# First layer of a three-way maximum network: seven half products in place of eight for seven of nine pairs of feature blocks

## The chip, the cores and the metric

The kernel runs on one core of one Trainium2 chip. The metric is the device time of one execution in microseconds (us); shorter is better. TensorE multiplies; VectorE (DVE), ScalarE (ACT) and GpSimd (POOL) do the elementwise work; SyncE (SP) issues the loads and stores.

## What is computed

```python
# q, k, v: 2 x 8 heads x 768 tokens x 64; local causal window of 96 tokens and 8 global tokens
scores = where(keep, q @ k.T / 8 - slope * dist, -1e9)
x = softmax(scores) @ v                       # 1536 tokens x 512
# first layer: three weights of 512 x 768, then 768 x 512
h = maximum(maximum(x @ w1, x @ w2), x @ w3)
x = h @ w_out
# gated layer: root mean square norm, two weights of 512 x 1536, then 1536 x 512
xn = x / sqrt(mean(x * x) + 1e-6) * rms_g
out = (silu(xn @ w_gate) * (xn @ w_val)) @ w_out2
```

The weights arrive in 64-bit floating point. Each number is held as a high and a low part, so every product of two blocks is three matmuls: low weight by high token, high by low, high by high.

## The kernel before

The 1536 tokens are two batches of 768, cut into four chunks of 384 columns (`C2`) for the first layer. The weights of a layer are cut into blocks of 128 features; a block holds 512 inputs as four pieces of 128 (`KT`).

**Attention** (`FastAttention.steps`) runs in 24 units of two heads by 256 queries. One step j of the loop issues for several units at once: the scaling of unit j+2 on POOL, the low part of unit j-1 (`out(..., True)`, a subtraction on DVE), scores of unit j+3 and transposes of unit j+1 on TensorE, the exponentials (maximum on DVE, exponential on ACT), the values of unit j on TensorE, and the high part of unit j (`out(..., False)`, ACT). PE, DVE, ACT and POOL keep the program's order here (`manual(FRONT)`). Into each step `fast` puts half units of the first layer (six matmuls: half of the 512 inputs of one weight block by one chunk), from step 12 on two in a step, and `w.pace` puts pieces of the conversion of weights.

**Weights** (`Weights`) are fetched by SP, turned from 64-bit to 32-bit by a scaling on ACT (`scaled`) and three bit operations on DVE (`bits`), and then either split into high and low (`split`, ACT and POOL) or kept whole for the gated layer (`pair`), where `operand` makes the sums of half blocks (DVE), their high part (ACT) and low part (POOL). `pace` advances this by one piece, and stops where the ring of `RING` split blocks is full.

**First layer** (`first`, `firsts`): for each block of 128 hidden features and each chunk, the products with the three weights come one after the other; the first is copied into `h1` by ACT, the two others enter by a maximum on DVE. Blocks 0 and 1 are begun inside attention, the rest follows in `behind`.

**Rows** (`rows`, `row_stage`, `square`, `power`, `scale`, `norm`): for each of 12 tiles of 128 tokens, 18 matmuls give the output product, ACT squares and sums it, DVE and POOL make the inverse root, DVE scales, TensorE transposes, and `norm` makes the operands of the gated layer in `xb`, seven of them for two tiles: Strassen's sums of tokens (features in halves, tokens in halves of a batch).

**Gated layer** (`gated`, `second`, `chained`): each pair of a gate block and a value block is one 2 x 2 block product by seven half products. `chained` sums them in three accumulators of two banks; DVE, ACT and POOL add, apply silu and multiply. `order` is written out by hand, and operands are made seven products ahead. A last product follows (`group_stage`, `stage`, `last`, `store`). In `behind` only TensorE keeps the program's order; DVE, ACT and POOL are ordered by a planner there.

## Time and profile before

| | us |
|---|---|
| median of 3 runs | 573.3 (572.76 to 573.45) |
| the profiled execution | 573.58 |
| its span, from the first to the last instruction | 571.8 |
| TensorE busy | 561.8 |
| DVE busy | 343.3 |
| ACT busy | 267.0 |
| POOL busy | 244.1 |

The table is read so: the span is what the profile covers, and the profiled execution's own time is 1.78 us more. Busy times of different engines overlap. A large busy share alone doesn't say what bounds a stage; for that the stages are read one by one.

### The profile page before, as it was taken

To read this page: it belongs to the slowest core of one execution; us is meant where nothing else is said; L and a number is where in the kernel's file an instruction comes from. 1 tells how busy PE (TensorE), PEld (TensorE's weight loads), DVE (VectorE), ACT (ScalarE), POOL (GpSimd) and SP (SyncE) were. 2 spreads that over 40 slices of the span, in tenths; PEclk is the share of its full clock that TensorE was granted. 3 is DMA by queue.
4 is the path that set the end of the run, shared out by engine and by line. 5 is a ranking of instruction groups with operands and counts; after the bars stand their busy time and mean duration, and the time that the engine had idled before them with its cause. 6 is when DMAs were issued, how large, how long until landed. Compare 5 with 4: busy or idle time off the path is not lost.

```text
span 571.8 us, 9171 instructions
## 1 busy us (share of the span) xinstructions
PE 561.8 (98%) x3324; PEld 508.8 (89%) x3324; DVE 343.3 (60%) x757; ACT 267.0 (47%) x628; POOL 244.1 (43%) x301
## 2 busy tenths in 40 slices
PE   8999999999999999999999999999999999999995
PEld 3778788899999999988899999999999998888884
DVE  5999889628679412267778555555556459752220
ACT  3888776514344001165755455555554546442210
POOL 4556554305155001057646666666666526420000
PEclk9999999999999999999999999999999999999999
DMA  8666663202535300000000222222222205303001
GB/s 297 192 207 225 216 216 105 80 1 80 179 83 190 97 1 0 1 2 1 1 0 1 75 73 75 76 73 75 75 73 75 73 1 155 104 2 128 33 24 42
DMA packets 15894, 48.72 MB, mean 85 GB/s; under 512 B 2016, under 2 KB 2016, under 8 KB 15840
## 3 DMA queue, kind: packets, MB, share of 16 engines
q1 hardware_dynamic: 15840, 48.05, 26.2%
q8 instruction: 28, 0.46, 0.3%
q14 instruction: 26, 0.21, 0.1%
HBM read 44.90 MB, written 3.15 MB: 84 GB/s over the span
## 4 chain that ended last, share of the span: by engine, by line
PE 90%; DVE 4%; ACT 3%; issue 1%; DMA 1%; POOL 0%; SPq 0%; DVEq 0%; ACTq 0%
PE c L574 28%; PE mm L379 27%; PE acc L638 17%; PE mo L426 8%; PE sc L844 3%; PE tr L885 3%; PE av L908 3%; ACT s L861 2%; DVE s L857 1%; PE tr L460 1%; DMA qk<-qk 1%; PE idle L369 1%; DVE xt L919 0%; DVE g L517 0%; ACT xb L464 0%
## 5 line engine op out<-in xcount | busy, mean ns | idle before, releaser
L574 PE MATMUL c<-xb,op 128*128 128x384 f32 x924 | 160.4, 334 | 0.2 <-DVE g L517 0.2
L574 PEld LDWEIGHTS c<-xb,op 128*128 128x128 f32 x924 | 160.1, 188 | 0.5 <-POOL op L254 0.5
L379 PE MATMUL mm<-xt,w 128*128 128x384 f32 x864 | 157.7, 338 | 0.0
L379 PEld LDWEIGHTS mm<-xt,w 128*128 128x128 f32 x864 | 148.5, 188 | 2.6 <-issue 2.6
L168 POOL TENSOR_TENSOR w<-x,w 128x512 fp32r<-128x512 f32 x36 | 51.8, 1441 | 79.7 <-ACT w L165 71.2
L875 POOL TENSOR_SCALAR s<-s,rs 128x232 f32<-128x232 f32 (+1 forms) x96 | 42.3, 459 | 37.5 <-DVE rs L870 27.7
L396 DVE TENSOR_TENSOR h<-mm,h 128x384 f32<-128x384 f32 x48 | 26.5, 553 | 46.9 <-PE mm L379 46.7
L426 PE MATMUL mo<-w,rst 128*128 128x512 f32 x216 | 52.1, 395 | 0.0
L861 ACT ACTIVATE s<-s,nmx 128x232 f32<-128x232 f32 (+1 forms) x96 | 44.5, 466 | 13.1 <-DVE nmx L857 12.8
L254 POOL TENSOR_TENSOR op<-s,op 128x256 fp32r<-128x256 f32 x48 | 38.1, 796 | 29.2 <-ACT op L253 28.0
L638 PE MATMUL acc<-w,gst 128*128 128x512 f32 x216 | 49.2, 389 | 0.0
L638 PE MATMUL acc<-w,st 128*128 128x512 f32 x216 | 49.1, 389 | 0.0
L638 PEld LDWEIGHTS acc<-w,st 128*128 128x128 f32 x216 | 40.6, 188 | 8.4
L638 PEld LDWEIGHTS acc<-w,gst 128*128 128x128 f32 x216 | 40.5, 188 | 8.4
L426 PEld LDWEIGHTS mo<-w,rst 128*128 128x128 f32 x216 | 39.8, 188 | 8.0
L588 POOL TENSOR_TENSOR h<-h,g 128x768 f32<-128x768 f32 x20 | 36.9, 1846 | 12.3 <-ACT g L607 10.0
L254 POOL TENSOR_TENSOR op<-x,op 128x256 fp32r<-128x256 f32 x36 | 29.1, 812 | 22.2 <-ACT op L253 22.2
L857 DVE CUSTOM_DVE_ANT_0 s<-sc,bias 128x232 f32<-128x232 f32 (+1 forms) x96 | 31.9, 376 | 6.8 <-PE sc L844 5.3
L610 DVE TENSOR_TENSOR h<-c,h 128x768 f32<-128x768 f32 x11 | 10.5, 958 | 41.9 <-PE c L574 41.9
L165 ACT CAST w<-x 128x512 fp32r<-128x512 f32 x36 | 22.2, 619 | 22.7 <-DVE x L151 14.6
L394 ACT COPY h<-mm 128x384 f32<-128x384 f32 x24 | 11.3, 472 | 42.4 <-PE mm L379 42.2
L844 PE MATMUL sc<-qk 64*128 64x232 f32 (+1 forms) x192 | 27.8, 379 | 2.4 <-DVE nmx L857 1.0
(114 smaller groups left out, 745.0 us busy)
## 6 DMA issues: line engine op xcount, KB each, us to landing
raw<-wgv SPq DMA_DIRECT2D x24, 512.0 KB, 3.8
raw<-w SPq DMA_DIRECT2D x18, 512.0 KB, 3.7
raw<-wo SPq DMA_DIRECT2D x18, 512.0 KB, 3.7
qk<-qk SPq DMA_DIRECT2D x24, 312.0 KB, 4.0
v<-vwin SPq DMA_DIRECT2D x10, 512.0 KB, 5.5
out<-o SPq DMA_DIRECT2D x12, 256.0 KB, 2.1
v<-vwin SPq DMA_DIRECT2D x2, 256.0 KB, 4.9
gcol<-gcol SPq DMA_DIRECT2D x1, 2.0 KB, 1.7
```

Source lines behind the costliest of these rows:

```text
L168: self.nc.gpsimd.tensor_tensor(out=t[:, 1, :], in0=self.x.pop(i), in1=t[:, 0, :], op=ALU.subtract)
L254: nc.gpsimd.tensor_tensor(out=t[:, 1, :], in0=s, in1=t[:, 0, :], op=ALU.subtract)
L379: self.nc.tensor.matmul(ps, w[:, wi, k * P:(k + 1) * P], x[b][:, k, xi, c0:c0 + C2], start=(i == 0), stop=(i == 3 * KT - 1),)
L396: self.nc.vector.tensor_tensor(out=h, in0=ps, in1=h, op=ALU.max)
L426: self.nc.tensor.matmul(ps, h[:, k % 3, hi, :], w[:, wi, :], start=(k + x == 0), stop=(k == NF1 - 1 and x == 2),)
L574: nc.tensor.matmul(two[:, b, :C2], a[:, wi, k * P:(k + 1) * P], self.xb[b][:, j, k, xi, :], start=(i == 0 and j in (0, 1, 5)), stop=(i == ...
L588: nc.gpsimd.tensor_tensor(out=o, in0=o, in1=y, op=ALU.mult)
L638: self.nc.tensor.matmul(ps, of(si), w[:, wi, :], start=(f == LAST[0] and si == 1), stop=(f == LAST[-1] and si == 0 and wi == 0),)
L844: nc.tensor.matmul(sc[j][:, i, :n], qk[r, i * P:(i + 1) * P], qk[r, k0:k0 + n], start=True, stop=True)
L857: nc.vector.tensor_tensor_reduce(out=s[:, j, :n], in0=self.sc[d][j][:, i, :n], in1=self.bias(n, 2 * pr + j), scale=-QK, scalar=3.0e38, op0 ...
L861: nc.scalar.activation(s[:, j, :n], s[:, j, :n], AF.Exp, bias=nmx[:, j:j + 1], scale=-1.0, accum_out=sm[:, i, j:j + 1])
L875: nc.gpsimd.tensor_scalar(s[:, j, :n], s[:, j, :n], rs[:, i, j:j + 1], 1.0, op0=ALU.mult, op1=ALU.mult)
```

## The change

In the first layer, four weight blocks of the first two feature blocks (the first two of the three weights) stay as plain products. The remaining weights are taken by pairs of neighbouring feature blocks: seven pairs, each a 2 x 2 block product (features in two blocks, inputs in halves, tokens in halves of a batch) by seven half products, in the same chained form that the gated layer has (`chained`, `sums1`). The sums of tokens that they need are made on chip from a 32-bit copy of attention's result (`xf`, `places`, `mix`, `mix_split`): for batch 0 during attention, for batch 1 behind it. `out` copies attention's result to `xf` on DVE, and its low part is now subtracted by POOL. The sums of half weight blocks for these pairs are made by POOL. FILL gives the half units per attention step, PACES the pieces of conversion per pair. The weights of the output product come in between (`couple`). The whole first layer keeps the program's order on all four engines. The first gated pairs' weights are now converted during the rows.

```diff
-RING = 9
+RING = 4
+NPLAIN = 2
+FILL = [0] * 12 + [1, 1, 2] * 4 + [2] * 4
+NA = 7
+PACES = [6, 14, 6, 6, 14, 8, 0]
...
     def pair(self, i):
+        f = self.units[i][0][1]
+        self.blocked = len(self.held) == 2
+        while self.blocked:
+            yield
+            self.blocked = len(self.held) == 2
+        self.held.add(f)
...
-            nc.vector.tensor_tensor(out=s, in0=x, in1=y, op=op)
+            (nc.gpsimd if -NA < f < 0 else nc.vector).tensor_tensor(out=s, in0=x, in1=y, op=op)
...
+        self.firstly = [(f, w) for f in range(0, NF1, 2) for w in range(NPLAIN if f == 0 else 0, 3)]
+        for n, (f, w) in enumerate(self.firstly):
+            for x in range(2):
+                u.append((("w1", n - NA, x), io["w123"][f + x, w], "op"))
+            for k in {3: (0, 1), 6: (2, 3, 4, 5)}.get(n, ()):
+                u.append((("wo1", k), io["wo1"][k], "wo1"))
...
-        for w in range(3):
+        for w in range(NPLAIN):
...
+    def tokens(self, j, b, k, x):
+        if j in (2, 3, 6):
+            if x == 0:
+                return self.thi[b][:, (2, 3, 6).index(j), k, :]
+            return self.xlo[b, j][:, k, :]
+        r, h = {0: (0, 0), 1: (1, 0), 4: (1, 1), 5: (0, 1)}[j]
+        return self.xt[b][:, 2 * r + k, x, h * C2:(h + 1) * C2]
+
+    def mix(self, b, j, eng):
+        q = self.xf[b]
+        o, x, y = {
+            3: ((0, 0), (0, 1), (0, 0)), 5: ((0, 1), (1, 1), (0, 1)),
+            2: ((1, 1), (1, 1), (0, 0)), 6: ((1, 0), (1, 0), (1, 1)),
+        }[j]
+        eng.tensor_tensor(out=q[o], in0=q[x], in1=q[y], op=ALU.subtract)
+
+    def mix_split(self, b, j, eng=None):
+        o = self.xf[b][MIXED[j]]
+        hi = self.xt[b][:, :2, 0, C2:] if j == 5 else self.thi[b][:, (2, 3, 6).index(j)]
+        if eng is None:
+            self.nc.scalar.copy(hi, o)
+            return
...
+        eng.tensor_tensor(out=lo, in0=o, in1=hi, op=ALU.subtract)
...
                 for wi, xi in ((1, 0), (0, 1), (0, 0)):
+                    x = self.tokens(j, b, k, xi) if f < 0 else self.xb[b][:, j, k, xi, :]
...
+    def sums1(self, n, j, ps):
...
+        if j == 0:
+            nc.scalar.copy(held(1), ps)
+        elif j == 1:
+            nc.vector.tensor_tensor(out=held(1), in0=ps, in1=held(1), op=ALU.add)
+            most(1)
+        elif j == 2:
+            nc.scalar.copy(held(2), ps)
+        elif j == 3:
+            nc.scalar.copy(held(3), ps)
+        elif j == 4:
+            if w == 0:
+                nc.scalar.copy(best[4], ps)
+            else:
+                nc.vector.tensor_tensor(out=best[4], in0=ps, in1=best[4], op=ALU.max)
+        elif j == 6:
+            nc.vector.tensor_tensor(out=held(2), in0=ps, in1=held(2), op=ALU.add)
+            most(2)
+        if j == (5 if last else 3):
+            nc.vector.tensor_tensor(out=held(3), in0=self.chain[n, 5][:, :, :C2], in1=held(3), op=ALU.add)
+            most(3)
...
+    def begin(self):
+        z, self.n_op = -1, 0
+        self.order = [(-NA, 0), (-NA, 1), (-NA, 2), (-NA, 5), (-NA, 3)]
+        for o in range(1 - NA, z):
+            self.order += [(o, 0), (o - 1, 4), (o - 1, 6), (o, 1), (o, 2), (o, 5), (o, 3)]
+        self.order += [(z, 0), (z - 1, 4), (z, 2), (z - 1, 6), (z, 3), (z, 5), (z, 1), (z, 6), (z, 4)]
+
+    def strassen(self):
...
+        for n, _ in enumerate(self.firsts(NC2 - 1)):
+            for fn, *args in todo[n]:
+                fn(1, *args)
+            if n % 2 and self.n_op < 7:
+                self.next_op()
...
+        for n, (o, j) in enumerate(self.order):
+            later.step()
+            for b, _ in enumerate(self.chained(o, j)):
+                if b == 0:
+                    self.next_op()
...
+                w.pace(paces - done)
...
+            if (o, j) == (-1, 1):
+                self.row_part(0, 0)
+        w.need(("wo1", NF1 - 1))
+        self.row_part(0, 1)
+        later.flush()
...
-    def out(self, d, low):
+    def out(self, d, part):
...
+        if part == 0:
+            nc.scalar.copy(o[:, 0], av)
+            for q, n, i in self.places(b, pr, c):
+                nc.vector.tensor_copy(q, av[:, i * P:i * P + n])
+        elif last:
+            nc.vector.tensor_tensor(out=o[:, 1], in0=av, in1=o[:, 0], op=ALU.subtract)
         else:
+            for q, n, i in self.places(b, pr, c):
+                a = slice(i * P, i * P + n)
+                nc.gpsimd.tensor_tensor(out=o[:, 1, a], in0=q, in1=o[:, 0, a], op=ALU.subtract)
...
-                            w.pace(1 + (r >= WMORE) + (r >= WMOST))
+                            w.pace(1 + (r in (8, 9, 10, 12, 14, 16)))
+                        if r >= len(FILL) - 5:
+                            body.next_op()
+                        for fn, j, eng in mixes.get(r - LEAD, ()):
+                            fn(0, j, eng)
```

`mixes` gives the four mixes of batch 0 to POOL at units 14 to 17, their high parts to ACT and their low parts to DVE (two) and POOL (two) at units 14 to 24; `todo` gives the mixes of batch 1 to DVE, and the splits to ACT, DVE (three of the low parts) and POOL (one). In `sums1`, `most` is a maximum between two tiles in SBUF on DVE, left out for the first weight of a block pair, and split by batch for the last pair.

## Rows read from the trace of the kernel before

**Rows 1.** The page's busy times: us, share of the span, instructions of each engine.

```profile
PE 561.8 (98%) x3324; PEld 508.8 (89%) x3324; DVE 343.3 (60%) x757; ACT 267.0 (47%) x628; POOL 244.1 (43%) x301
```

**Rows 2.** The chain of waits in order of time: start us, us, engine, line.

```profile
118.12 119.63 PE mm L379 x689
...
237.75 8.21 PE mo L426 x36
...
307.31 160.40 PE c L574 x924
```

**Rows 3.** Busy time by stage: stretch, its length, busy us, TensorE clock, DMA.

```profile
237.75:287.50 49.75, 49.75 (x239) 41.07 (x239) 30.14 (x67) 29.79 (x74) 30.16 (x29) 1.00 0.00 1
...
45.20:118.12 72.92, 72.92 (x600) 60.18 (x600) 58.21 (x194) 46.80 (x154) 34.77 (x62) 1.00 0.46 155
118.12:237.75 119.63, 119.63 (x691) 119.63 (x691) 63.15 (x96) 32.34 (x63) 30.21 (x24) 1.00 0.25 76
19.00:45.20 26.20, 25.05 (x241) 19.50 (x240) 24.65 (x103) 23.27 (x82) 14.49 (x32) 1.00 0.59 183
```

**Rows 4.** The same chain of waits, one full step of attention.

```profile
85.85 0.98 PE sc L844 x8
86.84 1.02 PE tr L885 x8
87.86 1.05 PE mm L379 x6
88.91 1.03 PE av L908 x16
89.94 1.24 PE mm L379 x6
```

**Rows 5.** Instructions by line and shape, DVE: count, busy us, mean ns, idle before.

```profile
L145 DVE SCALAR_TENSOR_TENSOR x<-raw,x 128x512 int32<-128x512 int32 x30 | 23.1, 774 | 0.6
...
L610 DVE TENSOR_TENSOR h<-c,h 128x768 f32<-128x768 f32 x11 | 10.5, 958 | 41.9 <-PE c L574 41.9
...
L919 DVE TENSOR_TENSOR xt<-av,xt 128x256 fp32r<-128x256 f32 x24 | 9.6, 399 | 5.5 <-ACT xt L921 5.5
...
L478 DVE TENSOR_SCALAR z<-tr,gcol 128x128 f32<-128x128 f32 x12 | 3.9, 340 | 0.0
...
L647 DVE COPY o<-acc 128x256 f32<-128x256 f32 x1 | 0.4, 425 | 13.6 <-PE acc L638 13.6
```

**Rows 6.** The same view, POOL.

```profile
L168 POOL TENSOR_TENSOR w<-x,w 128x512 fp32r<-128x512 f32 x36 | 51.8, 1441 | 79.7 <-ACT w L165 71.2 <-DMA raw<-wo 8.5
...
L254 POOL TENSOR_TENSOR op<-s,op 128x256 fp32r<-128x256 f32 x48 | 38.1, 796 | 29.2 <-ACT op L253 28.0
L588 POOL TENSOR_TENSOR h<-h,g 128x768 f32<-128x768 f32 x20 | 36.9, 1846 | 12.3 <-ACT g L607 10.0 <-DVE h L610 2.3
L875 POOL TENSOR_SCALAR s<-s,rs 128x232 f32<-128x232 f32 x80 | 36.7, 477 | 25.6 <-DVE rs L870 20.3 <-PE tr L885 5.3
```

**Rows 7.** Single lines, DVE: duration in ns, shortest, median and longest.

```profile
L151 DVE SCALAR_TENSOR_TENSOR x<-raw,x x30: 677/691/1669, 28.3 to 188.2; 128x512 int32<-128x512 int32 x30
L151 DVE SCALAR_TENSOR_TENSOR x<-raw,xs x30: 675/687/689, 314.4 to 503.7; 128x512 int32<-128x512 int32 x30
...
L621 DVE TENSOR_TENSOR gst<-h,gst x12: 949/957/1808, 462.4 to 505.5; 128x768 fp32r<-128x768 f32 x12
```

**Rows 8.** The timeline where the rows begin: start us, us, engine, line.

```profile
241.91 0.60 ACT L439 ACTIVATE x<-mo 128x512 f32<-128x512 f32 x1 [1.52 <-PE mo L426]
...
242.49 0.50 ACT L413 CAST rst<-h 128x384 fp32r<-128x384 f32 x1
...
243.45 0.75 DVE L450 TENSOR_SCALAR x<-mo,ri 128x512 f32<-128x512 f32 x1 [0.67 <-POOL ri L446]
...
244.50 0.56 DVE L415 TENSOR_TENSOR rst<-h,rst 128x384 fp32r<-128x384 f32 x1 [0.29 <-ACT rst L413]
...
245.79 0.60 PE L460 MATMUL tr<-ident,x 128*128 128x128 f32 x4
```

More of the change, by code (lines that the diff above doesn't have):

```diff
@@ L173, in everything @@
             self.fetch(i)
-        two = [i for i, u in enumerate(self.units) if u[2] == "op"]
-        yield from self.convert(0, two[0])
-        for i in two[::2]:
-            yield from self.pair(i)
-        yield from self.convert(two[-1] + 1, len(self.units))
+        a, n = 0, len(self.units)
+        while a < n:
+            place = self.units[a][2]
+            if place == "op":
+                yield from self.pair(a)
+            elif place == "wo1":
+                yield from self.couple(a)
+            else:
+                z = a
+                while z < n and self.units[z][2] not in ("op", "wo1"):
+                    z += 1
+                yield from self.convert(a, z)
+                a = z - 2
+            a += 2
     def convert(self, a, z):
@@ L396, in part @@
                 self.nc.vector.tensor_tensor(out=h, in0=ps, in1=h, op=ALU.max)
-        for w in range(3):
+        for w in range(NPLAIN):
             self.weights.need(("w1", f, w))
             self.later.step()
-            ps = yield from self.product(("w1", f, w), self.xt, c, f"mm_{f}_{c}_{w}")
+            bank = None
+            if c == NC2 - 1 and f == 1 and w == 1:
+                bank = self.twos[2].tile([P, 2, 512], F32, tag="m2", name="mm2")[:, 0, :C2]
+            ps = yield from self.product(("w1", f, w), self.xt, c, f"mm_{f}_{c}_{w}", bank)
@@ L417, in row_stage @@
-        self.rst[t] = st
+            self.row_part(t, x)
     def rows(self, t):
-        ps = self.bank(f"mo_{t}")
+        ps = self.single(f"mo_{t}")
         for k in range(NF1):
@@ L490, in second @@
         nc, later = self.nc, self.later
-        nm, n = f"{f}_{b0}_{j}", b1 - b0
+        nm = f"{f}_{b0}_{j}"
         a = self.weights["op", f, j]
-        two = self.two_banks("q_" + nm) if n == 2 else None
         for b in range(b0, b1):
             later.step()
-            ps = two[:, b, :C2] if two is not None else self.bank("q_" + nm, C2)
+            ps = self.single("q_" + nm, C2)
             i = 0
@@ L613, in chained @@
-        self.later(1, ready)
+        if j == 0:
+            g = self.ev["g1", f] = self.evp.tile([P, B, C2], F32, tag="ev", name=f"g1_{f}")
+            nc.scalar.copy(g, ps)
+        elif j == 1:
+            g = self.ev["g1", f]
+            nc.vector.tensor_tensor(out=g, in0=ps, in1=g, op=ALU.add)
+            nc.scalar.activation(g, g, AF.Silu)
+        elif j == 2:
+            nc.scalar.copy(h[:, 0], ps)
+        elif j == 3:
+            nc.scalar.copy(h[:, 1], ps)
+        if j == (5 if last else 3):
+            c = self.chain[f, 5][:, :, :C2]
+            nc.vector.tensor_tensor(out=h[:, 1], in0=c, in1=h[:, 1], op=ALU.add)
@@ L653, in store, with firsts @@
         self.nc.sync.dma_start(out=self.io["out"][t * P:(t + 1) * P, :], in_=o)
-    def firsts(self, f0, f1, c0, c1):
-        for f in range(f0, f1):
-            for c in range(c0, c1):
-                yield from self.first(f, c)
-    def behind(self):
-        w, later = self.weights, self.later
-        for _ in self.firsts(2, NF1, 0, NC2):
-            if ("x", 1) not in w.done:
-                w.pace()
-        later.flush()
+    def firsts(self, c):
+        for f in range(2):
+            yield from self.first(f, c)
@@ L1089, in fast @@
 def fast(tc, io, consts, nlf, ngf):
-    chunks = [(b, c) for b in range(B) for c in range(NCH)]
+    nc, chunks = tc.nc, [(b, c) for b in range(B) for c in range(NCH)]
     def manual(engines):
@@ L1108, in fast @@
+        body.begin()
+        with manual(FRONT):
+            with ExitStack() as c2:
+                body.warm_up(c2)
                 att = FastAttention(body, c2, Masks(tc, c2, nlf, ngf), chunks)
-                side, n_side, r = early(), 0, 0
+                side, r = early(), 0
                 for part in att.steps():
                     if part < 2:
-                        c = n_side // 12
                         for _ in range(WARMS[r] if r < len(WARMS) else 0):
                             body.keep_warm(r)
-                        if c < NC2 - 1 and r >= LEAD + 1 + NPAIR * -(-(c + 1) * C2 // CN):
-                            next(side)
-                            n_side += 1
+                        if part == 0:
+                            for _ in range(FILL[r]):
+                                next(side)
@@ L1124, in fast @@
+            body.open_behind()
+            body.strassen()
         with manual(BEHIND):
-            for n, _ in enumerate(side):
-                w.pace(n % 2)
-            for n, _ in enumerate(body.firsts(0, 2, NC2 - 1, NC2)):
-                w.pace(n % 2)
             body.behind()
@@ L1134, in general @@
 def general(tc, io, consts, nlf, ngf):
-    chunks = [(b, c) for b in range(B) for c in range(NCH)]
+    nc, chunks = tc.nc, [(b, c) for b in range(B) for c in range(NCH)]
     with ExitStack() as ctx:
```

323 lines of the change are left out of this document (211 added, 112 removed).

## The prediction

> **What bounds the kernel now.** I read the page's busy lines first, then the chain of waits in order of time, then the busy times by stage, and last the prices of single forms. TensorE is busy for 98% of the span [rows 1]. The chain shows the same as lengths: one unbroken run of first-layer matmuls from 118.12 to 237.75 us, then the rows of the first output product, and from 307.31 us one run of 160.40 us of half products for the gated layer [rows 2]; between the rows' end (287.5, [rows 3]) and that run lie some 20 us in which small steps alternate. So a matmul taken out of one of these runs shortens the span by its pitch, as long as nothing else becomes later. The reader should see two things in the stage table [rows 3]. TensorE is busy all the time from 45.2 us on, while DVE has 58.21 of 72.92 us in the second half of attention, 63.15 of 119.63 in the first layer and 30.14 of 49.75 in the rows: there is room, but not without end. And from 19.0 to 45.2 us DVE has 24.65 of 26.20 and ACT 23.27: there TensorE waits for them. The granted clock is 1.00 in these stages (its upper level, 2.4 GHz) and plays no part.
>
> **The matmuls taken out.** Before, 18 weight blocks x 4 token chunks x 12 matmuls are 864. After, four blocks stay plain (4 x 4 x 12 = 192) and seven pairs take 7 products x 2 batches x 6 = 84 each, 588: 780 in all, 84 fewer. Where do they leave? In the run after attention, 689 matmuls took 119.63 us [rows 2], 0.1736 us each; the gated layer's half products, which have the form that the new ones get (three two-bank accumulators, chained sums), took 160.40 us for 924, also 0.1736 [rows 2]. The form therefore costs nothing by itself. After: of 24 half units (six matmuls each) that FILL deals out, two come behind the last `av`, eight more belong to the last chunk, so 60 + 588 = 648 matmuls x 0.1736 = 112.5 us, 7.1 less than 119.6. Inside attention a full step is scores 0.98, transposes 1.02, half unit 1.05, values 1.03, half unit 1.24 [rows 4]; 29 half units lie before the last `av` now (689 of 864 matmuls come after it), 22 will, and 7 x (1.05 + 1.24)/2 = 8.0 us go. Together **-15.1 us**, a little more than 84 x 0.1736 = 14.6, because a half unit inside attention costs more than its pitch. This holds if TensorE stays the engine that is late everywhere. The rest is what takes that away.
>
> **Attention, first part (to 45 us).** DVE's subtraction for the low part (399 ns) becomes a copy to `xf`; the nearest rows are a copy of the same size out of PSUM at 425 ns and, for the third of the units whose tokens fall in two quarters, two of 340 ns [rows 5]. That is +0.03 or +0.28 us in a step of 3.4, some 0.9 us over nine steps that DVE bounds. The copy also waits for the values of its own step on TensorE, and the weight bits and the next reciprocal queue behind it. The subtraction goes to POOL at about 0.8 us [rows 6], behind the four scalings; POOL is at 14.49 of 26.20 us, so there is room. But a DVE operation with both sources in SBUF that meets a POOL operation stretches: 691 ns median against 1669 at most for one form of the bits [rows 7]. One pace fewer at step 11 gives back 0.6. Bounds 0 and +3 us; I take **+1.0**, near the counted copies, because ACT and DVE alternate there and one pays for the other.
>
> **Attention, second part.** A step with one half unit needs 0.98 + 1.02 + 1.05 + 1.03 = 4.08 us of TensorE in place of 5.32. DVE had 58.21 us for 72.92 there, 80% or 4.2 us of a 5.3 us step, with two or three paces in a step; a pace is about one bit operation (0.77, [rows 5]), so with one it needs some 3.4. ACT had 46.80 of 72.92 us [rows 3]. So TensorE stays just ahead. The four mixes on POOL (the form of 768 takes 1.85 us; [rows 6] has these prices) and the five first operands come on top, and POOL then has four scalings (4 x 0.48) + 0.80 + 1.85 = 4.6 us in steps of 4.1 to 5.1. Nothing waits for the mixes at once. Bounds 0 and +3 us; **+1.0**, for four steps in which POOL is a little long and its subtractions stretch DVE's bits.
>
> **The Strassen stage (102 us).** DVE, for a pair whose result goes through a maximum: three additions out of PSUM (958 ns, [rows 5]), one maximum out of PSUM and three between SBUF tiles, 7 x 0.958 = 6.7 us, and six bit operations with one side in PSUM (0.69 each, the second form of [rows 7]), 4.1: 10.8 of the pair's 84 x 0.1736 = 14.6 us. Over the stage: five such pairs' sums 33.5, two without maxima 5.7, sixteen converted blocks at 2.1 make 33: 72 of 102 us. POOL: 49 operand subtractions and 24 sums at 0.80 plus six at 1.44 [rows 6] make 67 us. Both fit. The tightest wait: product (o+1,1) starts in the bank that (o,4) filled, one product (12 x 0.1736 = 2.08 us) later; DVE needs 0.96 for that maximum and may have up to one 0.96 in front. It holds with little to spare. Bounds 0 and +6 (five pairs of 1.2 us, one stretched maximum each in front of such a release); **+1.0**, by the gated layer, whose run [rows 2] is the same chain without a pitch above 0.1736 us, but with fewer DVE sums.
>
> A row first: the 768-element subtraction between SBUF tiles takes 957 ns at the median and 1808 at most [rows 7], and the bits with one side in PSUM never over 689. The Trainium skill, "SBUF — State Buffer", section "Who interferes with whom", says that a DVE instruction with two SBUF inputs and a GpSimd one that reads SBUF exclude each other, the later one standing still until the other is done, and that one with a single SBUF input does not. The trace agrees. Read against this change: the fifteen new maxima and POOL's new sums are of the kind that collide; by it the stage would still fit, since 8.8 us of POOL (eleven at 0.80) and 2.9 of maxima laid end to end are 11.7 of 14.6 us.
>
> **The handovers.** The last chunk's mixes (four of about 0.96 on DVE) and their splits run under 60 + 24 matmuls (10.4 + 4.2 us) before the first mixed product needs them. At the end, tile 0's second half waits for (-1,6): addition 0.96 [rows 5], maximum 0.56, cast 0.50, subtraction 0.56 (the two last and, for the maximum, the same form: [rows 8]), and four changes of engine at some 0.2 us, my estimate: 3.4 us, under one product (2.08) and the first nine matmuls of the rows (about 2.1). Covered by 0.8 us. If that cover fails the wait is in the open. Bounds 0 and +2; **+0.5**.
>
> **The rows.** The blocks of the first two gated pairs and the operands of pair 0 were made during the first layer; now six blocks and seven operands are made during the rows. DVE: six blocks x 3 x 0.77 us and four sums of 0.4 (256 elements, [rows 5]) make 15.5, on 30.14 of 49.75 [rows 3]: 91%. The chain to see is from a row's matmuls to its transposes: square from 241.91, scaling from 243.45 for 0.75, transposes at 245.79 [rows 8]: 1.6 us of slack, with two DVE steps in it. One bit operation of 0.69 in front of each costs nothing; two stretched ones (1.67) cost 1.7 us in that tile. Behind the transposes stand 18 row matmuls on TensorE. Bounds 0 and +4; **+1.0**. SP's queue carries these blocks later too: sixteen loads in 102 us and six in the rows, against 3.8 us from issue to landing; no charge. The gap behind the rows and the two runs after it keep their instructions: 0, between -1 and +1 for the order around the last tile.
>
> **The sum.** -15.1 + 1.0 + 1.0 + 1.0 + 0.5 + 1.0 = -10.6 us. The profiled execution took 573.58 us (span 571.8), 0.28 above the median 573.3: 573.58 - 10.6 - 0.28 = **562.7 us**.
>
> **The rivals.** (1) *All of it is hidden.* For it: TensorE had no gap from 45 us to 287 although DVE was at 80% in one part. Against it: DVE near its limit before 45 us and in the rows. 573.3 - 15.1 = 558.2 us. Chance 0.18. (2) *Half is given back*: attention and the rows pay their upper bounds (3 + 3 + 4) and the rest half: 573.3 - 15.1 + 8 to 12, about 568 us. For it: the 24.65 of 26.20 us and the 91%. Chance 0.20. (3) *Slower*: DVE bounds the Strassen stage. Were every maximum at 1.81 us and every bit operation at 1.67 [rows 7], a pair would take 3.8 + 5.4 + 10.0 = 19.3 us in place of 14.6, five pairs +23.5: 573.3 - 15.1 + 23.5 = 582 us. It decides from 17.6 us per pair on, where the whole gain is gone. Against it: the bits have a side in PSUM there, and that form's maximum is 689 ns. The rule of the Trainium skill named above would give this only if both sides of the bits lay in SBUF. Chance 0.04. (4) *No change within 0.2%*: rival 2 with the stage's 6 us too. Chance 0.03.
>
> **How the numbers follow.** My forecast (560 to 565 us) has 0.55. The range runs from rival 1 to rival 2, 557.5 to 569 us, which leaves out the upper end of rival 2 and rivals 3 and 4. A difference under 0.2% can't be told from none here. Faster: 0.55 + 0.18 + 0.20 = 0.93; same 0.03; slower 0.04.
>
> **What would show it.** The first-layer lines should show 780 matmuls at the same pitch; the last `av` should end near 112 us (110.1 if the charges on attention are nothing), the first row matmul should start near 226, and the rows should last 50 to 51 us. A pitch above 0.174 us in the Strassen run with DVE named as releaser proves that step wrong; so does an attention that ends at 115 or later, or a gap of over 3 us where the rows begin. I would be most wrong if the collisions of POOL and DVE were common rather than rare.

## The result

The changed kernel is slower. Its executions took 576.6 to 579.3 us against a median of 573.33 before; the ratio is 1.0081, with a 95% interval of 1.0057 to 1.0106. (One further execution, in which the matmuls of both layers took 2.7 times their usual time, is left out.) A second set of executions has a median of 577.31 us, ratio 1.0077 (1.0051 to 1.0102); the profiled one of them took 577.37 us with a span of 575.6. The forecast was 562.7 us and the range ended at 569: the prediction was wrong, and on the wrong side.

The page's busy line of the changed kernel answers to [rows 1]: TensorE has 12 us less to do, and the span is 3.8 us longer.

```profile
PE 549.7 (96%) x3240; PEld 496.1 (86%) x3240; DVE 379.2 (66%) x788; ACT 293.1 (51%) x684; POOL 318.2 (55%) x397
```

Where did the time go? I cut the span at four points of TensorE's order: the end of attention's last values matmul (`av`), the first row matmul, the first half product of the gated layer (`q`), and the first of its chained run (`c`).

| stage, us | before | changed | difference | my sum |
|---|---|---|---|---|
| up to the last `av` | 118.12 | 118.40 | +0.3 | -8.0 + 2.0 |
| first layer from there | 119.47 | 114.97 | -4.5 | -7.1 + 1.5 |
| the rows | 54.22 | 62.08 | +7.9 | +1.0 |
| from there to the chained run | 15.50 | 15.48 | 0.0 | 0 |
| the rest | 264.49 | 264.67 | +0.2 | 0 |
| span | 571.8 | 575.6 | +3.8 | -10.6 |

Two lines of the table hold nearly the whole miss: attention kept none of its 8 us, and the rows lost 8 us. The busy times by stage of the changed kernel answer to [rows 3] (columns as there):

```profile
19.00:45.20 26.20, 21.57 (x194) 16.93 (x194) 21.34 (x87) 19.66 (x66) 16.13 (x33) 0.96 0.56 167
45.20:118.40 73.20, 68.73 (x601) 57.42 (x597) 56.92 (x201) 48.33 (x161) 53.05 (x93) 0.99 0.39 123
118.40:233.37 114.97, 113.32 (x649) 112.22 (x649) 83.73 (x105) 52.28 (x100) 74.29 (x80) 1.00 0.23 74
233.37:295.45 62.08, 55.79 (x261) 44.23 (x261) 52.32 (x103) 38.34 (x94) 40.59 (x38) 1.00 0.17 51
```

The reader should see what is strange in the first row. From 19.0 to 45.2 us TensorE has 21.57 us where it had 25.05, but DVE too has less, 21.34 in place of 24.65, and ACT less, 19.66 for 23.27. Nobody is busier but POOL (16.13 for 14.49): the engines wait for one another. In the rows DVE has 52.32 of 62.08 us, and TensorE waits for 6.3.

Who waits? This is the line of DVE's new copy to `xf` in the changed kernel: durations in ns (shortest, median, longest), then idle time of DVE ahead of it, in us and times.

```profile
L1131 DVE COPY xf<-av x32: 279/358/426, 18.8 to 118.9; 128x256 f32<-128x256 f32 x16, 128x128 f32<-128x128 f32 x16
...
  ACT xt L1129: 21.0, 24
```

DVE stood still before each of the 24 copies (in 32 pieces), 21.0 us in all, and not for TensorE's values but for ACT's cast of the same result. One step of the timeline shows why (start us, us, engine, line):

```profile
40.89 0.49 ACT L1070 ACTIVATE s<-s,nmx 128x232 f32<-128x232 f32 x1 [2.30 <-DVE nmx L1066]
...
41.55 1.37 PE L1053 MATMUL sc<-qk 64*128 64x232 f32 x8 [2.19 <-DVE nmx L1066]
...
42.33 0.47 ACT L1070 ACTIVATE s<-s,nmx 128x232 f32<-128x232 f32 x1
...
42.80 0.35 ACT L1129 CAST xt<-av 128x256 fp32r<-128x256 f32 x1
...
43.18 0.49 DVE L1131 COPY xf<-av 128x128 f32<-128x128 f32 x2 [0.76 <-ACT xt L1129]
...
43.58 0.42 DVE L148 TENSOR_SCALAR x<-x 128x512 int32<-128x512 int32 x1
44.04 0.69 DVE L150 SCALAR_TENSOR_TENSOR x<-raw,x 128x512 int32<-128x512 int32 x1
...
44.96 0.40 DVE L1066 CUSTOM_DVE_ANT_0 s<-sc,bias 128x232 f32<-128x232 f32 x1
```

ACT can begin its exponentials only when DVE has made the maxima. Its cast stands behind four of them. DVE's copy starts just behind the cast (43.15 and 43.18), the weight bits and the reciprocals queue behind the copy, and the next step's maxima behind those. DVE and ACT take turns, and the scores wait for the maxima, 2.19 us here. In this step one of the two bits ahead of the maxima was stretched as well (the fence under e2), so the 2.19 us aren't the copy's wait alone. In the kernel before, the subtraction that read this bank stood one step later on DVE, where the cast was mostly done: it waited for the cast in three of 24 steps.

```profile
  ACT xt L921: 5.5, 3
```

The Trainium skill, "PSUM — Partial Sum Buffer", section "PSUM bank collisions raise a hardware error", says that no two engines may touch one bank and partition quadrant at once, two readers included, and that the compiler orders them by a dependency. The trace agrees: each of the 24 copies starts some 0.03 us after the cast of its bank has ended, though both only read. The wait is 0.9 us per step here.

### The profile page after: what moved, and what is told of

Same layout as the page of the kernel before. It is cut to its first block, busy times and chain, and to the rows that moved or that the text cites. A ratio compares the mean times of both kernels' runs of the same rounds, so it can differ in the third digit from the quotient of the medians.

```text
span 1892.9 us, 9241 instructions
## 1 busy us (share of the span) xinstructions
PE 1885.4 (100%) x3240; PEld 1187.6 (63%) x3240; DVE 363.9 (19%) x788; ACT 294.4 (16%) x684; POOL 309.3 (16%) x397
## 4 chain that ended last, share of the span: by engine, by line
PE 100%; DVE 0%; ACT 0%; issue 0%; ACTq 0%
PE c L686 30%; PE acc L803 19%; PE mo L541 9%; PE mm L456 6%; PE av L1117 4%; PE tr L1094 4%; PE sc L1053 4%; PE q L614 3%; PE c_-7_0_1963 L686 2%; PE c_-2_0_2677 L686 2%; PE c_-1_0_2835 L686 2%; PE c_-3_0_2526 L686 2%; PE c_-6_0_2075 L686 2%; PE c_-5_0_2226 L686 2%; PE c_-4_0_2381 L686 2%; PE tr L575 1%
## 5 line engine op out<-in xcount | busy, mean ns | idle before, releaser
L686 PE MATMUL c<-xb,op 128*128 128x384 f32 x924 | 569.3, 889 | 0.0
L686 PEld LDWEIGHTS c<-xb,op 128*128 128x128 f32 x924 | 405.7, 439 | 163.2 <-issue 127.6
L541 PE MATMUL mo<-w,rst 128*128 128x512 f32 x216 | 182.9, 1106 | 0.0
L803 PE MATMUL acc<-w,gst 128*128 128x512 f32 x216 | 177.7, 1095 | 0.0
L803 PE MATMUL acc<-w,st 128*128 128x512 f32 x216 | 177.5, 1095 | 0.0
L541 PEld LDWEIGHTS mo<-w,rst 128*128 128x128 f32 x216 | 92.6, 431 | 77.8 <-issue 75.7
L456 PEld LDWEIGHTS mm<-xt,w 128*128 128x128 f32 x192 | 83.9, 442 | 31.3 <-issue 24.5
L1117 PE MATMUL av<-at,v 128*64 128x128 f32 (+1 forms) x352 | 74.0, 664 | 0.0
L1094 PE MATMUL tr<-ident,s 128*128 128x128 f32 x176 | 72.2, 605 | 0.0
L614 PE MATMUL q<-xb,op 128*128 128x384 f32 x84 | 52.8, 892 | 0.0
```

The costliest lines, as they stand in the source:

```text
L456: self.nc.tensor.matmul(ps, w[:, wi, k * P:(k + 1) * P], x[b][:, k, xi, c0:c0 + C2], start=(i == 0), stop=(i == 3 * KT - 1),)
L541: self.nc.tensor.matmul(ps, h[:, k % 3, hi, :], w[:, wi, :], start=(k + x == 0), stop=(k == NF1 - 1 and x == 2),)
L614: nc.tensor.matmul(ps, a[:, wi, k * P:(k + 1) * P], self.xb[b][:, j, k, xi, :], start=(i == 0), stop=(i == 5))
L686: nc.tensor.matmul(two[:, b, :C2], a[:, wi, k * P:(k + 1) * P], x, start=(i == 0 and j in (0, 1, 5)), stop=(i == 5), skip_group_check=True,)
L803: self.nc.tensor.matmul(ps, of(si), w[:, wi, :], start=(f == LAST[0] and si == 1), stop=(f == LAST[-1] and si == 0 and wi == 0),)
L1094: self.nc.tensor.transpose(tr[:, t, j, :], s[:, j, o:o + P], self.b.ident)
```

## The experiments

All edits are to the changed kernel. "Attention ends" is the end of the last `av`; "rows" run from the first row matmul to the first `q`; "behind the rows" goes on to the chained run.

| kernel | us | ratio to before | attention ends | rows | behind the rows | span |
|---|---|---|---|---|---|---|
| before | 573.3 | 1 | 118.12 | 54.22 | 15.50 | 571.8 |
| e0, as it is | 577.31 | 1.0077 (1.0051 to 1.0102) | 118.40 | 62.08 | 15.48 | 575.6 |
| e1, copy ahead of the cast | 571.19 | 0.9977 (0.9965 to 0.9989) | 112.74 | 62.11 | 15.49 | 569.4 |
| e2, low part by DVE | 573.84 | one execution | 116.69 | 61.58 | 15.49 | 572.0 |
| e3, rows' bits in PSUM | 575.58 | 1.0047 (1.0030 to 1.0063) | 118.89 | 57.98 | 17.40 | 573.8 |
| e4, rows without bits | 572.02 | one execution | 118.89 | 56.75 | 15.49 | 570.2 |
| e5, copy in the next step | 569.89 | 0.9942 (0.9920 to 0.9964) | 113.77 | 61.90 | 15.49 | 568.6 |
| e6, transposes later | 574.85 | 1.0035 (1.0021 to 1.0049) | 118.97 | 56.40 | 17.78 | 572.0 |
| e7, e1 and e6 | 569.13 | 0.9927 (0.9911 to 0.9944) | 114.08 | 56.95 | 17.77 | 567.9 |
| e8, no sums of tokens | 565.91 | one execution | 108.57 | 62.07 | 15.49 | 563.5 |
| e9, e5 and rows' bits in PSUM | 565.13 | 0.9855 (0.9838 to 0.9871) | 112.21 | 59.54 | 15.49 | 564.7 |
| e10, e9 and low part by DVE | 564.70 | 0.9852 (0.9836 to 0.9868) | 110.18 | 58.00 | 15.49 | 562.1 |
| e11, e10 and transposes later | 561.59 | 0.9795 (0.9779 to 0.9812) | 110.25 | 53.79 | 17.78 | 559.8 |

The ends of attention and of the rows are read from one profiled execution of each kernel. How far they can be off is seen where several kernels have the same attention: it ends at 118.40, 118.89, 118.89 and 118.97 us (e0, e3, e4, e6), at 112.74 and 114.08 (e1, e7), at 113.77 and 112.21 (e5, e9), and at 110.18 and 110.25 (e10, e11).

**The changed kernel as it is (e0).**

> The changed kernel as it is, for a profile of an undisturbed execution. Theory A (DVE and POOL collide in the Strassen stage): 575.9 us of span with a pitch above 0.1736 us per matmul in the first layer, spread over its products, and DVE named as releaser. Theory B (attention lost its cover): the last values matmul ends at 115 us or later and the Strassen stage keeps its pitch. Theory C (TensorE stands still somewhere long enough that the granted clock falls): one or two gaps of some us, and behind them a stretch of matmuls at half the clock; the mean clock is 0.99 against 0.998 before, so some 5 us of the span would be lost to the clock alone.

Measured: the rows above. Theory A fails: the Strassen stage keeps its pitch (below). Theory B holds in its first half, the last `av` ends at 118.40. Theory C is a side effect: the granted clock is 0.96 in the stretch up to 45.2 us and 0.994 over the span, and costs some 1.7 us at most (last section), not 5. None of the three had named the rows.

**The copy ahead of the cast (e1).** The same instructions, two statements changed over.

```diff
         if part == 0:
-            nc.scalar.copy(o[:, 0], av)
             for q, n, i in self.places(b, pr, c):
                 nc.vector.tensor_copy(q, av[:, i * P:i * P + n])
+            nc.scalar.copy(o[:, 0], av)
```

> Undoes one wait: the copy of attention's result to xf stands ahead of ACT's cast of the same bank, so DVE no longer waits for the cast (21.0 us in 24 waits in the changed kernel, the cast standing behind four exponentials); the instructions are the same. Theory W (this wait makes DVE and ACT take turns in attention): the last values matmul ends at 110 to 113 us in place of 118.4, and the time falls by 5 to 8 us, to 569 to 572. Theory C (POOL's new subtractions stretch DVE's bits): 117 us or later, within 1.5 us of the changed kernel.

Attention ends at 112.74 us, 5.7 earlier, and the time falls by 6.1 to 571.19. No instruction was taken away, only the order on one bank changed, so the wait cost that. (From e6 to e7, which differ by the same edit, attention ends 4.9 us earlier.) In the waits between 19 and 118 us (engine and line waiting, what it waited for: us, times, longest) the releasers have changed:

```profile
ACT xt L1131 <- DVE xf L1130: 12.0, 13, 3.0
DVE xf L1130 <- PE av L1117: 11.3, 12, 1.8
```

Now the copy waits for the values on TensorE, which my prediction had named, and ACT for the copy.

**The low part back on DVE (e2).**

```diff
-        nc, last = self.nc, d == self.n - 1
+        nc, last = self.nc, True
```

> Undoes another part: the low part of attention's result is subtracted by DVE out of PSUM again, not by POOL; the copy to xf stays behind ACT's cast. Theory W: DVE has 0.4 us more per step and the wait stays, so the last values matmul ends 2 to 8 us later than 118.4. Theory C: POOL's 18 us of subtractions are gone and the bits fall back to 0.7 us, so it ends 3 to 6 us earlier.

Attention ends at 116.69, 1.7 us earlier than in e0, although DVE has one more operation per step and still waits 19.1 us for the cast. My theory W alone expected it later; theory C expected 3 to 6 us. So POOL's new subtractions cost too, as the smaller part. How they cost it is not shown. The stretched bits of theory C are there: of the 24 bit operations between 19 us and the end of attention, six took 5.1 us more in all than the usual 0.42 or 0.69, and in e2 none is stretched. But three of the six started while POOL made the low part of a weight block, which the kernel before does too, and three beside a mix; none started beside a new subtraction. The changed kernel's timeline has one of the first three, 1.52 us in place of 0.69:

```profile
37.66 1.29 POOL L170 TENSOR_TENSOR w<-x,w 128x512 fp32r<-128x512 f32 x1
...
37.98 1.52 DVE L150 SCALAR_TENSOR_TENSOR x<-raw,x 128x512 int32<-128x512 int32 x1
```

**The rows' bits with one side in PSUM (e3).**

```diff
-        self.weights.psx = None
...
-        self.singles = [... bufs=2 ... for n in range(3)]
+        self.singles = [... bufs=2 ... for n in range(2)]
+        self.weights.psx = e(tc.tile_pool(name="psr", bufs=2, space=PSUM, side="right"))
```

> The blocks converted during the rows have one side of their bit operations in PSUM (two banks taken from the rows' six), as in the Strassen stage. Theory RC (DVE's bits and POOL's operations collide in the rows): the bit operations return to 0.69 us and the stretch from the first row matmul to the gated run's start falls from 77.4 us to 70 to 73. Theory RL (the eighteen bit operations are too many for DVE's queue whatever each takes): 75 us or more.

The stretch from the first row matmul to the chained run is 75.4 us, which by its wording is theory RL's; its parts say that RC holds in the rows. The rows fall by 4.1 us to 57.98; behind them 1.9 are lost, where the half products have four banks in place of six. The bits by line and shape in the rows (count, busy us, mean ns, idle before), first in the changed kernel, then in e3:

```profile
L156 DVE SCALAR_TENSOR_TENSOR x<-raw,x 128x512 int32<-128x512 int32 x6 | 6.0, 998 | 0.0
...
L148 DVE TENSOR_SCALAR x<-x 128x512 int32<-128x512 int32 x6 | 4.6, 760 | 0.9 <-ACT x L139 0.9
L150 DVE SCALAR_TENSOR_TENSOR x<-raw,x 128x512 int32<-128x512 int32 x6 | 4.5, 753 | 0.0
```

```profile
L150 DVE SCALAR_TENSOR_TENSOR xs<-raw,xs 128x512 int32<-128x512 int32 x6 | 4.1, 681 | 0.0
L148 DVE TENSOR_SCALAR xs<-xs 128x512 int32<-128x512 int32 x6 | 4.0, 686 | 0.0
L156 DVE SCALAR_TENSOR_TENSOR x<-raw,xs 128x512 int32<-128x512 int32 x6 | 4.0, 672 | 0.0
```

15.1 us of bits become 12.1. In the changed kernel's timeline seven of the eighteen start while POOL works on tiles of 256 to 512 columns, and these seven take 0.96 to 1.50 us; the eleven others take 0.41 to 0.69. Two of one form:

```profile
235.35 0.42 DVE L148 TENSOR_SCALAR x<-x 128x512 int32<-128x512 int32 x1
...
238.77 2.03 POOL L298 TENSOR_TENSOR op<-x,op 128x256 fp32r<-128x256 f32 x2 [1.06 <-ACT op L297]
...
239.25 0.96 DVE L148 TENSOR_SCALAR x<-x 128x512 int32<-128x512 int32 x1
```

L150 and L156 have two sources in SBUF. They are of the kind that the prediction names from the Trainium skill, "SBUF — State Buffer", section "Who interferes with whom", and with one source in PSUM they are at 681 and 672 ns. L148 has one source, in SBUF, and is stretched all the same. The prediction's "one with a single SBUF input does not" leaves out a condition: in the Trainium skill, the same section, it holds outside DVE's two-port modes, and a `tensor_scalar` is among the operations that can enter them. No run here shows which mode L148 had. With its source in PSUM it takes 686 ns, more than it does undisturbed in SBUF. What the prediction took as rare is common in the rows.

**The rows without bits (e4).** The bit operations of the blocks converted there are left out; all else is done. It is a kernel for its time alone.

```diff
+        if self.plain:
+            if part == 2:
+                del self.raws[i]
-        if part == 0:
+        elif part == 0:
```

> Leaves out the bit operations of the blocks converted during the rows (these weights are then wrong); loads, scalings and operands stay. Both theories of the rows: the rows take 50 to 52 us in place of 62, and the stretch up to the gated run 69 to 71. If the rows stay at 58 or more, it is not the bits but the operands' casts and POOL's subtractions that hold the rows up.

The rows take 56.75 us, not 50 to 52: that expectation rested on my misreading of the rows' length (below). Of the 7.9 us lost against the 54.22 of before, 5.3 are gone with the bits and 2.5 stay. The timelines show where: ahead of the first tile's transposes. From the first row matmul to these it was 8.20 us before, 11.92 in the changed kernel and 10.65 here; from there to the end of the rows 46.02, 50.16 and 46.10. These first transposes in the changed kernel and in e4 (before: [rows 8]):

```profile
245.29 0.66 PE L575 MATMUL tr<-ident,x 128*128 128x128 f32 x4 [2.10 <-DVE x L565]
```

```profile
243.83 0.66 PE L578 MATMUL tr<-ident,x 128*128 128x128 f32 x4 [1.27 <-DVE ms L562]
```

In that stretch of e4 DVE has the last maximum of the first layer, sums for operands, and subtractions of the first tiles' rows that take up to 1.38 us where the undisturbed one takes 0.56. Which of them holds the first tile up wasn't tried.

**The copy in the next step (e5).** The copy stands where the subtraction stood in the kernel before.

```diff
         if part == 0:
             nc.scalar.copy(o[:, 0], av)
-            for q, n, i in self.places(b, pr, c):
-                nc.vector.tensor_copy(q, av[:, i * P:i * P + n])
-        elif last:
+            return
+        for q, n, i in self.places(b, pr, c):
+            nc.vector.tensor_copy(q, av[:, i * P:i * P + n])
+        if last:
```

> The copy to xf is moved into the next step on DVE, behind the reciprocals, where ACT's cast of the same bank is long done and the values are too; the instructions are the same. With the copy ahead of the cast DVE still waited 11.3 us for the values and ACT 12.0 us for DVE. Theory W (it is waits between DVE and ACT on the shared bank that cost attention its cover): the last values matmul ends at 110 to 112 us, and the time is 568 to 571. If what is left there is POOL's and DVE's load and not a wait: 112.5 us or later, no better than with the copy ahead of the cast (571.2).

569.89 us, but attention ends at 113.77 in the profiled execution, later than with the copy ahead. There the granted clock was 0.95 between 45.2 and 80 us; in e9, which has the same attention, it was 1.00 and attention ended at 112.21. By its time theory W holds, by the end of attention the other. So this way is no worse than e1 and no clear step beyond it. The wait for the cast is nearly gone, 2.0 us in all (1.3 in e9): what is left in attention is not this wait.

**The transposes one tile later (e6).**

```diff
-                if n == 2 and t:
-                    self.norm(t - 1)
+                if n == 2 and t > 1:
+                    self.norm(t - 2)
...
-            if j == 2:
-                self.norm(NT // P - 1)
+            if j in (0, 2):
+                self.norm(NT // P - 2 + j // 2)
```

> The rest as in the changed kernel, but each tile's transposes stand one tile later on TensorE (the tile before last in place of the last), the last two inside the first half products of the gated layer. Theory RL (the rows are late only because the scaled row comes late behind DVE's and POOL's queues, while their work fits on average): the rows fall from 62.1 us to 55 to 57, the time by 4 to 6 us to 571 to 573. Theory RT (DVE or POOL has too much work in the rows altogether): the rows stay at 60 or more, or what they gain is lost before the gated run starts.

The rows fall to 56.40 us (one tile's four transposes, 0.45 us, have gone behind them), and 2.3 us are given back behind them, where these transposes now stand and TensorE waits 1.30 us for the last tile's scaled row. The profiled span is 3.6 us shorter, the median 2.5. So theory RL holds for the rows, but its gain in time (4 to 6 us) did not come. In the changed kernel's waits from 233 to 296 us, this is what had held the rows up:

```profile
PE tr L575 <- DVE x L565: 5.4, 5, 2.1
POOL ri L561 <- DVE ms L559: 5.0, 4, 2.2
DVE x L565 <- POOL ri L561: 4.3, 4, 1.6
PEld tr L575 <- DVE x L565: 4.3, 3, 2.5
```

TensorE stands at the transposes because the scaled row is late; the inverse root on POOL is late because the mean on DVE is, behind bits; and behind the transposes stand 18 row matmuls. With a whole tile more of slack, most of it vanishes: the work fits on average, but not in the 1.6 us of slack of [rows 8].

**Both (e7).** The edits of e1 and e6 together.

> The copy to xf ahead of ACT's cast and the transposes one tile later, together: if the two losses are separate, their gains add up (6 from the first, what the late transposes give alone): 565 to 567 us, faster than the kernel before by 6 to 8.

569.13 us, not 565 to 567. I had added e6's gain as I expected it; with the measured ones (6.1 + 2.5) the sum is 568.7, so the two losses are separate as far as these times can tell.

**No sums of tokens (e8).** The copies to `xf`, all mixes and splits are left out, the low part is subtracted by DVE, and the three mixed products read unmixed tokens. It is a kernel for its time alone.

```diff
-            for q, n, i in self.places(b, pr, c):
-                nc.vector.tensor_copy(q, av[:, i * P:i * P + n])
...
     def mix(self, b, j, eng):
+        return
...
     def mix_split(self, b, j, eng=None):
+        return
```

> Leaves out everything that the sums of tokens add: the copies to xf, the mixes and their splits; the low part is subtracted by DVE out of PSUM, and the three mixed products read unmixed tokens (their results are wrong, their matmuls the same). It shows what attention and the handover would be by TensorE's own count: the last values matmul at 110 to 111 us, as my sum of steps had it, and the first row matmul 112.5 to 114 us later. If attention ends later than 112 without any of this work, the step of my sum that took 8.0 us out of attention was wrong by itself.

Attention ends at 108.57, earlier than the 110 to 111 expected; the first row matmul comes 112.85 us later, as expected, and the rows still take 62.07. So the count of TensorE's steps did not fail (it had said 110.1, 1.5 us too late). All that attention lost came with the sums of tokens, 9.8 us by this one execution, at most some 1.7 of them through the clock (last section), and the rows' loss has nothing to do with them. The four ends of the last `av`, each from its kernel's timeline: changed, e1, e2, e8.

```profile
117.30 1.10 PE L1117 MATMUL av<-at,v 104*64 104x128 f32 x16
```

```profile
111.64 1.10 PE L1117 MATMUL av<-at,v 104*64 104x128 f32 x16
```

```profile
115.59 1.10 PE L1117 MATMUL av<-at,v 104*64 104x128 f32 x16
```

```profile
107.47 1.10 PE L1115 MATMUL av<-at,v 104*64 104x128 f32 x16
```

**Three versions put together (e9 to e11).** e9 has the copy in the next step (e5), and the rows' bits in PSUM (e3) with the two banks handed back to the half products when the rows end:

```diff
+        while ("x", 2) not in w.done:
+            w.pace()
+        self.psr_only.close()
+        w.psx = None
+        self.singles.append(... name="m12", bufs=2 ...)
```

> The copy to xf in the next step, and the blocks of the rows converted with one side in PSUM; these two banks go back to the half products when the rows end (kept until the gated run, their lack cost 1.9 us there). Theory RC (stretched bits are most of what the rows lose): the rows take 57 to 58.5 us in place of 62, the stretch behind them is 15.5 again, and the time falls by 3.5 to 4.5 from 569.9 to 565.5 to 566.5. Theory RL (the queue alone): 568.5 or more.

565.13 us, 4.8 less than e5: theory RC, and a little more than its 3.5 to 4.5. Behind the rows it is 15.49 again. The rows took 59.54 in the profiled execution, 1.0 above RC's range, and the clock accounts for that: over them the granted clock was 0.97, where e10, with the same rows, had 1.00 and 58.00. Their rows in the view of [rows 3], first e9, then e10:

```profile
225.13:284.67 59.54, 56.27 (x262) 45.75 (x261) 48.69 (x103) 37.41 (x93) 37.90 (x38) 0.97 0.17 54
```

```profile
223.73:281.73 58.00, 54.72 (x262) 44.56 (x261) 48.33 (x103) 37.23 (x93) 38.15 (x38) 1.00 0.18 55
```

e10 adds the edit of e2 to e9:

> The same, and the low part of attention's result subtracted by DVE out of PSUM again, so POOL has 18 us less in attention and DVE 0.4 us more per step. If the collisions with POOL are what is left of the loss in attention (113.8 against 108.6 without the sums of tokens), the last values matmul ends at 111 to 112.5 and the time falls by another 1.5 to 2.5; if it is DVE's load, it ends at 114 or later and the time rises.

Attention ends at 110.18, two us earlier than in e9 and 1.6 later than in e8: with the wait gone, POOL's subtractions are some half of what was left. Again it isn't their collisions with the bits: in e9 seven stretched bits cost 2.4 us, all beside a new subtraction, in e10 six cost 4.9 beside other work of POOL, and attention is shorter. The median falls by only 0.4 us and the intervals of e9 and e10 overlap, so on the whole time this edit isn't settled. The profiled spans differ by 2.6 us, but e9's is its longest execution and e10's its shortest. e11 adds the edit of e6 to e10:

> The same, and each tile's transposes one tile later. If the stretched bits were the whole reason for late transposes, nothing is left to gain and the two norms behind the rows cost up to 2.3 us: 0 to +2 us against the kernel without it. If DVE's queue still holds the transposes up, the rows fall by another 1.5 to 3 us and the time by 0 to 1.

561.59 us: 3.1 less by the medians and 2.3 by the profiled spans, where I expected no more than 1. The rows fall by 4.2 us to 53.79 and 2.3 come back behind them. The transposes had still been held up by DVE's queue, though the bits no longer stretched (674 to 686 ns in e10). In e10 this line stood in the waits of the rows:

```profile
PE tr L576 <- DVE x L566: 3.3, 2, 2.7
```

In e11's rows TensorE is busy throughout, 53.79 of 53.79 us:

```profile
223.73:277.52 53.79, 53.79 (x257) 44.32 (x257) 47.77 (x94) 35.74 (x91) 37.83 (x38) 1.00 0.18 60
```

e11 beats both kernels: 0.9795 of the time before (0.9779 to 0.9812), and some 15.7 us less than the changed kernel.

## Why the prediction was wrong

**The matmuls taken out: right.** 84 fewer at the same pitch. With the sums of tokens away, attention ended at 108.57 and the stage behind it took 112.85 us (e8), against 110.1 and 112.5 by the steps.

**Attention, both parts: the step that failed first.** The prediction saw that the copy adds a wait and named what queues behind it, but took its releaser to be the values on TensorE, and put the wait at nothing: the charge is that of the copies' own length and of stretched bits. The releaser is ACT's cast, by the order on one bank. Both parts together were charged 2.0 us, bounds 0 to 6; the wait cost 5.7 (e1; 4.9 from e6 to e7), and attention lost 8.3 against the 110.1 of the steps. The copy's own price was right or high: a whole block took 425 ns as forecast, two halves 0.49 us where 0.68 was counted. POOL's subtractions cost 1.7 us beside the wait (e2) and 2.0 without it (e9 to e10), both by the ends of attention; that was in the bounds, but not by the stretched bits that the prediction named. To set DVE's 3.4 us against a step of 4.08 compares sums of busy time and cannot see a loop through two engines in order: 21.0 us of waits at low busy shares.

**The Strassen stage: right in kind, a little small in size.** It was charged 1.0, and the handovers 0.5; the stage lost 2.5 us against its 112.5. The run holds 2.08 us per product but for two places, and the maxima take 957 to 1207 ns: rival 3 did not happen. The largest single wait was one that I had not listed, at the fifth product, 1.17 us: ACT's copy of the bank that this product writes stands behind the cast of an operand whose sum POOL has not finished. The copy ended at 139.06; the profile names POOL's subtraction for the same operand, which ended at 139.17. Which of the two held the product isn't settled, and both stand behind POOL's late sum. The timeline of the changed kernel:

```profile
137.96 0.41 ACT L297 CAST op_-6_2_2016<-s_-6_2_2014 128x256 fp32r<-128x256 f32 x1 [3.20 <-POOL s_-6_2_2014 L277]
...
138.27 0.79 ACT L726 COPY u_-7_2_2026<-c_-7_0_1963 128x768 f32<-128x768 f32 x1
138.44 0.73 POOL L298 TENSOR_TENSOR op_-6_2_2016<-s_-6_2_2014,op_-6_2_2016 128x256 fp32r<-128x256 f32 x1 [0.52 <-ACT op_-6_2_2016 L297]
...
139.21 0.41 PE L686 MATMUL c_-7_0_1963<-th,op_-7_3_1843 128*128 128x384 f32 x1 [1.17 <-POOL op_-6_2_2016 L298]
```

The handover to the rows was to be covered by 0.8 us. It was not: TensorE waited 0.67 and 0.26 us for DVE's subtractions of the first rows, and ahead of these stood two scalings of weights on ACT (1.25 us) and three bit operations on DVE. The table counts this as rows. The 0.2 us for a change of engine was high: from ACT to DVE it is 0.03 in the 24 copies.

**The rows: the second step that failed, and a misreading with it.** The kernel before's rows end not at 287.5 us but at 291.81. The chain of waits leaves TensorE at 287.50, because the work that ended last runs through the norm of a tile, and I took that for the end of the rows; the twelfth tile's matmuls come after it. The right stretch of before, in the view of [rows 3]:

```profile
237.59:291.81 54.22, 54.22 (x261) 44.74 (x261) 33.94 (x78) 31.47 (x78) 30.71 (x30) 1.00 0.00 1
```

The gap behind it is therefore 15.5 us, not 20. That alone does no harm to the sum, since the rows were charged as a difference. The charge was what failed: +1.0 with a bound of +4, measured +7.9. The mechanism stood in the text (two DVE steps in a chain with 1.6 us of slack, bits in front of them). It was priced by the median of the bits, 0.69 us, and at 1.7 us for a tile with two stretched ones: the charge is less than one such tile, the bound between two and three. In the rows the bits took 753 to 998 ns on average, and DVE was at 84% of a stage that had become longer; TensorE waited five times for the scaled row, at most 2.1 us. Of the 7.9 us, 3.7 lie ahead of the first tile's transposes and 4.1 behind. By the experiments 4.1 go with the stretching (e3) and 5.3 with the bits as a whole (e4); a tile more of slack takes back 5.2, not counting the moved transposes (e6). These shares overlap; they are ways to remove the same waits. The 2.5 us that stay without bits all lie ahead of the first tile's transposes; what they are made of, operands or POOL, stays open.

**The rivals and the range.** The outcome lies beyond rival 2, whose upper bounds for attention (6) and for the rows (4) were each below what was measured (8.3 and 7.9). Rival 2's own sum was wrong as well: the terms that it names, 3 + 3 + 4 and half of the stage's 6 and the handovers' 2, make 14 and not 8 to 12, so 572.2 us in place of about 568, and the range's upper end of 569 came from it. All the bounds together, 18 us, would have meant 576.2, slower than before. Rivals 3 and 4 needed the Strassen stage for that; the two losses alone, 16.2 us, take back the whole 15.1.

## What to carry to other kernels

When an edit adds a second reader of a PSUM bank on another engine, look at where the first reader stands in its own queue: the new one waits for that place, however early the data is there. A mean busy share of 80% says nothing about a loop that runs through two in-order engines, nor about a chain with 1.6 us of slack; price the chain with the operations stretched as they are in the busiest stretch, not at the median. And a change that takes work from the bounding engine by giving it to others should be tried with the added work left out: that one run (e8) told which losses were its own.

## What was not expected of the hardware

TensorE's clock falls within attention in the changed kernel. TensorE waited 2.19 us up to 41.55; the eight transposes that follow took 1.67 us where the next eight take 1.09, and the sixteen values 1.98 where they take 1.10 later. Between 44 and 46 us the granted clock was 0.50, the lower of the clock's two levels (1.2 of 2.4 GHz); with 0.80 and 0.84 in the two us before and behind, some 1.7 us are lost, an estimate from these three shares. TensorE there, and the two us at 0.50:

```profile
41.55 1.37 PE L1053 MATMUL sc<-qk 64*128 64x232 f32 x8 [2.19 <-DVE nmx L1066]
42.85 1.67 PE L1094 MATMUL tr<-ident,s 128*128 128x128 f32 x8
44.45 1.98 PE L1117 MATMUL av<-at,v 104*64 104x128 f32 x16
...
47.46 1.09 PE L1094 MATMUL tr<-ident,s 128*128 128x128 f32 x8
```

```profile
44.00:46.00 2.00, 2.00 (x17) 1.67 (x17) 1.93 (x11) 1.31 (x5) 0.79 (x2) 0.50 0.48 152
```

It doesn't fall in every execution of the same instructions. e5 and e9 have the same attention and ran alike up to a wait of 1.48 and 1.47 us. Behind it e5 was granted 0.50 between 50 and 52 us and e9 1.00; the next values start 1.48 us later in e5, and attention ends 1.56 later. First e5, then e9:

```profile
47.56 1.20 PE L1053 MATMUL sc<-qk 64*128 64x128 f32 x8 [1.48 <-DVE nmx L1066]
48.69 1.76 PE L1094 MATMUL tr<-ident,s 128*128 128x128 f32 x8
...
52.30 1.11 PE L1117 MATMUL av<-at,v 104*64 104x128 f32 x16
```

```profile
47.60 1.20 PE L1060 MATMUL sc<-qk 64*128 64x128 f32 x8 [1.47 <-DVE nmx L1073]
48.73 1.09 PE L1101 MATMUL tr<-ident,s 128*128 128x128 f32 x8
...
50.82 1.10 PE L1124 MATMUL av<-at,v 104*64 104x128 f32 x16
```

In the rows it was e9 that fell, to 0.57 between 246 and 250 us behind a wait of 2.73 us, and e10 that didn't behind the same wait. A wait on another engine can thus cost some 1.5 us more than its own length, and differently from run to run.
